# The first batch's softmax reciprocals turned from one repeated column instead of from a wide copy

## The chip, the cores and the metric

One core of one Trainium2 chip. The metric is device time in microseconds (us) of one execution. Lower is better. The engines are named as in the profile: PE is TensorE's products, PEld its weight loads, DVE is VectorE, ACT is ScalarE, POOL is GpSimd, SP is SyncE, which here only issues DMAs.

## The reference, cut to what matters

Three stages follow one another on 4 batches of 576 rows: attention with 8 heads of 64 columns, a gated feed-forward layer (the MoE names), and a spatial gating layer. The change lies in the attention alone:

```python
scores = scale * np.matmul(q_rot, k_rot.transpose(0, 1, 3, 2))
scores = scores - np.max(scores, axis=-1, keepdims=True)
attn = np.exp(scores)
attn = attn / (np.sum(attn, axis=-1, keepdims=True) + 1e-09)
return np.matmul(attn, v).astype(np.float32)
```

The division by the row's sum is what matters here. The kernel does not divide the exponentials. It multiplies the finished product with v by the reciprocals of the sums.

## The kernel before, in words

**Units.** The attention is cut into 72 units, 18 for each batch and 9 for each four heads. An ordinary unit m is 128 rows of the queries for two heads. Units 4, 13, 22 and so on (m % 9 == 4) are tails: the last 64 rows of four heads. So the first batch is units 0 to 17, of which 4 and 13 are tails and 16 are ordinary.

**One unit, step by step** (function `unit`, line 314). PE forms the scores into PSUM (`scores`, L347, or L339 and L336 from the second batch on). DVE takes the negated row maximum of each of two heads (`top`, L351). ACT takes the exponentials with the row's sum beside them (`expo`, L356, two of them). ACT adds 1e-9 (`total`, L360), and DVE takes the reciprocals (`norm`, L363), two numbers for each of 128 rows, in `sm[:, 3, :]`. ACT then copies each reciprocal 64 times side by side into a 128 x 128 tile `rb` (`spread`, L367). PE transposes the exponentials into PSUM in two halves of 8 (`turn`, L376). ACT copies these to SBUF (`take`, L404, two of them). `turn_rest` transposes the rest, into a PSUM tile `u`: the last 128 columns of exponentials (L389) and the wide tile of reciprocals (L390). In a tail it is 8 small products against the identity instead (L386), 4 of them on reciprocals. DVE copies the result to SBUF (`take_rest`, L411, L409 in a tail). When two ordinary units, or a tail, are complete, PE multiplies by v (`values`, L418), and DVE multiplies that by the turned reciprocals (`gather`, L430).

**Two kinds of ordinary units.** After units 1, 6, 8, 10, 15 and 17 the product with v follows directly; call these value units. After the ten others (0, 2, 3, 5, 7, 9, 11, 12, 14, 16) the next unit's transposes follow; call these plain units.

**What sets the order.** The order of all instructions on each engine is written by a list scheduler in the kernel (class `Plan`, line 52). Each step has an engine, a planned cost, the steps that it waits for, a delay after them (0.12 unless given) and a rank. A step on PE whose kind differs from the one before costs 0.10 more (`SWITCH`). The planned costs around the change: `scores` 1.07, `top` 0.75, `expo` 0.93, `total` 0.20, `norm` 0.17, `spread` 0.26, each half of `turn` 0.27, each `take` 0.59 with 0.05 between, `turn_rest` 0.22 (0.55 in a tail), `take_rest` 0.42, `values` 2.3 or 2.9. ACT also converts weights (L169, L180) between these, and DVE does weights (L165 to L174) and the rotation of q and k (L258, L266).

**Fillers.** Up to the planned time 125, the planner puts products of the identity with itself, whose results nobody reads, into gaps that it sees on PE (`filler`, L678):

```python
n = min(int((t - begin - FILL_MARGIN) / FILL_US), FILL_MOST)
```

with a margin of 0.30, 0.22 for one filler product and at most 20 of them. In the trace one filler product is two instructions. The number is fixed when the kernel is built: on the chip PE executes all of them, whether or not it would have waited.

**After the first batch** the feed-forward layer of the batch before (`feed`, L514, L553) shares PE with the attention of the next, and from about 500 us the later stages (L699, L763) follow.

Of the kernel before, what the change touches and what calls it, by code (L numbers as in the profile page):

```python
# [22 lines left out]
NFC = DF // 128  # L23
NU = B * 18
NFIRST = 2
EXACT = NP
WB, GB, WB2, GB2 = 3, 2, 3, 2
RAW, ROT, VB, PFB, PTB, XTS = 2, 4, 2, 3, 2, 6
# [5 lines left out]
HEAD = slice(0, 64), slice(64, 128)  # L34
# [17 lines left out]
class Plan:  # L52
# [5 lines left out]
    def add(self, eng, us, fn, deps=(), rank=0.0, after=0.12, take=None, give=None, port=False, kind=None):  # L58
        s = Step(eng, us, fn, deps, rank, after, take, give, port, kind)
        self.steps.append(s)  # L60
        return s
# [52 lines left out]
def body(ctx: ExitStack, tc, qp, kp, vp, cs, mu_k, mu_r, w_k, w_v, w_r, w_in, w_sp, b_sp, w_out, out):  # L114
    nc = tc.nc
# [21 lines left out]
    ident = const.tile([128, 128], F32, name="ident")  # L137
# [77 lines left out]
    add = plan.add  # L215
# [5 lines left out]
    ropes, vloads, exps, turned, valued, xdone, stored = {}, {}, {}, {}, {}, {}, {}  # L221
# [23 lines left out]
    def prep(i):  # L245
# [5 lines left out]
        for z, k in [(z, k) for z in sides for k in (1, 0)]:  # L251
# [8 lines left out]
            def rope(k=k, z=z):  # L260
                x = t["raw", k]
                if i >= EXACT:
                    t[k] = x[:, 0, :]
# [11 lines left out]
            def low(k=k):  # L275
                t["lo", k] = at.tile([128, S], F32R, tag="rl", bufs=ROT, name=f"rl{i}_{k}")
                nc.vector.tensor_tensor(t["lo", k], t[k], raw(t["hi", k]), op=ALU.subtract)
                if k == 0:
# [11 lines left out]
                    need - 2.5, port=True)  # L290
            if i < EXACT:
                ropes["n", n] = done[z.start, k] = add("DVE", 0.15 + 0.62 * part, rope, [a] + last, need - 2.5, port=True)
# [21 lines left out]
    def unit(m):  # L314
        w = which(m)
        tail = len(w) == 2
        st = units[m] = {}
        g, k = divmod(m, 9)
# [5 lines left out]
        def scores(halves=(0, 1)):  # L324
# [3 lines left out]
            ps = st["s"]  # L328
            if w[0][0] >= EXACT:
                for u, (i, c) in enumerate(w):  # L330
# [38 lines left out]
        def turn(n, slot=None):  # L369

            if n == 0:
                st["t"] = ps_t.tile([128, 2, 8, 64], F32, tag="t", name=f"t{m}")
            for c in range(4):
                for h, r in enumerate(HEAD):
                    k = 64 * (h if tail else n) + 128 * c
                    nc.tensor.transpose(st["t"][:, h, 4 * n + c, :], st["p"][r, n, k:k + 128], ident[r, r])  # L376

        def turn_rest(slot):

            pt, p = ps_m.tile([128, 4, 128], F32, tag=f"m{slot}", name=f"u{m}"), st["p"]  # L380
            st["u"] = pt
            if tail:
                for u in range(2):
                    for k in range(2):
                        for j, r in enumerate(HEAD):
                            nc.tensor.matmul(pt[r, u, HEAD[k]], st["r"][r, u, :] if k else p[r, u, 512 - 512 * j:576 - 512 * j],  # L386
                                             ident[r, r], start=True, stop=True)
            else:
                nc.tensor.transpose(pt[:, 0, :], p.rearrange("p a b -> p (a b)")[:, 512:640], ident)  # L389
                nc.tensor.transpose(pt[:, 1, :], st["r"].rearrange("p a b -> p (a b)"), ident)  # L390

        def turned_to(u):
            d = into[u if tail else 0]
# [4 lines left out]
        def take(k):  # L398
            o = turned_to(k)
            if tail:  # L400
                o = o[:, 0:8, 256:320].rearrange("p (h c) q -> p h c q", h=2)
            else:
                o = o[:, 4 * k:4 * k + 4, 128 * part:128 * part + 128].rearrange("p c (h q) -> p h c q", h=2)
            nc.scalar.copy(o, st["t"][:, :, 4 * k:4 * k + 4, :])  # L404
# [38 lines left out]
                             m - 0.5)  # L443
        t = add("ACT", 0.2, total, [exps[m, 1]], m - 0.3)
        nm = add("DVE", 0.17, norm, [t], m - 0.3)
        sp = add("ACT", 0.26, spread, [nm], m - 0.3)
        late = [y for d in into for y in freed.get(d["n"] - PTB, [])]
        t = add("PE", 0.27, lambda slot: turn(0), [exps[m, 0]], m + -0.02, take="t", kind="s")
        turned[m, 0] = x = add("PE", 0.27, lambda: turn(1), [exps[m, 1], t], m + 0.05, kind="s")
        x = add("ACT", 0.59, lambda: take(1), [x] + late, m - 0.2, 0.05)  # L450
        x = add("ACT", 0.59, lambda: take(0), [x] + late, m - 0.2, give=t)
        turned[m, 1] = t = add("PE", 0.55 if tail else 0.22, turn_rest, [sp], m + 0.2, take="m", kind="t")
        y = add("DVE", 0.55 if tail else 0.42, take_rest, [t] + late, m - 0.2, give=t)
        for d in into:
            d["ev"] += [x, y]
        if part and k != 3 or tail:
# [3 lines left out]
            x = add("DVE", 0.49 if duo["cols"] > 256 else 0.42, gather, [v] + mixed.get(i - XTS, []), m + 0.5, give=v)  # L460
# [130 lines left out]
    for c in (0, 2, 4, 6, 1, 3, 5, 7, *range(8, 16)):  # L591
        k = c < 8
# [6 lines left out]
    for m in range(NU):  # L599
        for i, _ in which(m):  # L600
            while i not in ropes:
                prep(len(vloads))
        unit(m)
        for n, args in enumerate(early):
            if m == EARLY + int(EVERY * n):
                weight_steps(weight_early(*args), m + 12, [scored[m]])
        for i in range(B * NP):
            if i not in ropes and i >= ROT // 2 and max(which_last(i - ROT // 2)) <= m:
                prep(i)
        if m % 18 == 17:  # L610
            if m == NU - 1:
                second["close"] = close = add("SP", 0.0, lambda: open_second(), [x for x in plan.steps if x not in fed], 74, 0.1)
            n = len(plan.steps)
            for h in range(2):
                feed(m // 18, h)
            fed.update(plan.steps[n:])
# [101 lines left out]
    def receptance_raw(b, e, r):  # L718
        ps = wide(f"r{b}_{e}")
        sl = slice(e * 128, (e + 1) * 128)  # L720
        product(ps, [(wr[w][:, c, sl], xr[a][:, c, :]) for c in range(NP) for a, w in PARTS])
        nc.scalar.activation(two_half(r), two_bank(ps), AF.Sigmoid)
        return r

    firsts = {(0, e): receptance_raw(0, e, stage[0].tile([128, S], F32, tag=f"rr{e}", name=f"rr0_{e}"))
              for e in range(NFIRST)}
    ph1.close()
# [192 lines left out]
```

## Time and profile before

| | us |
|---|---|
| median of 3 runs | 767.26 (766.88 to 768.66) |
| the profiled execution's own time | 766.66 |
| its span | 764.9 |
| PE busy | 748.1 (98%) |
| DVE busy | 474.8 (62%) |
| ACT busy | 457.0 (60%) |

The span is the time between the first and the last instruction in the profiled execution. A busy PE is not a PE that does useful work: fillers count as busy.

### The profile page before, as it was taken

Reading aid. Unit: us, or ns where it says so; the run is one execution under the profiler, and the core shown is the slowest. Engines: PE = TensorE matmul, PEld = TensorE weight load, DVE = VectorE, ACT = ScalarE, POOL = GpSimd, SP = SyncE. Lnnn points to the kernel's source line nnn. Section 1 sums busy time; section 2 is a strip of 40 time slices with the busy share of each in tenths; the row PEclk is TensorE's granted clock in tenths of the full one; section 3 lists DMA queues with packets and bytes.
Section 4 is the critical chain, followed back from the end, with each engine's and each line's share of the span. In section 5 each row is a group of like instructions: output and inputs, shape, how many; then the busy total and the mean of one; then the engine's idle time right before and its main releaser. Section 6 shows DMA issues by size and latency. Waiting matters only on the chain.

```text
span 764.9 us, 15911 instructions
## 1 busy us (share of the span) xinstructions
PE 748.1 (98%) x6530; PEld 668.0 (87%) x6530; DVE 474.8 (62%) x881; ACT 457.0 (60%) x1045; POOL 109.0 (14%) x132
## 2 busy tenths in 40 slices
PE   8999999999999999999999999999999999999998
PEld 8777778798788888888798799999989999998997
DVE  5878888988977986886866445256363342545111
ACT  4678788887887877878877555236334232523221
POOL 2242434102121121022031000002020000101000
PEclk9999999999999999999999999999999999999999
DMA  8444541442461552443351067182202112010101
GB/s 292 149 131 145 178 132 49 146 135 81 151 211 27 182 178 93 152 144 117 108 184 45 18 215 248 63 272 70 63 1 82 44 47 78 17 32 1 63 1 63
DMA packets 35275, 84.23 MB, mean 110 GB/s; under 512 B 4545, under 2 KB 10433, under 8 KB 35202
## 3 DMA queue, kind: packets, MB, share of 16 engines
q1 hardware_dynamic: 34658, 82.63, 32.9%
q8 instruction: 51, 0.84, 0.5%
q10 hardware_dynamic: 544, 0.59, 0.3%
q14 instruction: 22, 0.18, 0.1%
HBM read 60.65 MB, written 22.55 MB: 109 GB/s over the span
## 4 chain that ended last, share of the span: by engine, by line
PE 92%; DVE 3%; ACT 3%; DMA 1%; issue 0%; POOL 0%; ACTq 0%; POOLq 0%
PE mv L553 13%; PE mk L514 13%; PE v L418 11%; PE sp L699 8%; PE r L699 7%; PE u L699 7%; PE hv L763 7%; PE o L699 7%; PE t L376 6%; PE s L339 5%; PE s L347 2%; ACT pt L404 2%; PE u L389 1%; PE s L336 1%; DMA raw<-qp 1%; PE I-119_120 L678 1%
## 5 line engine op out<-in xcount | busy, mean ns | idle before, releaser
L351 DVE TENSOR_REDUCE sm<-s 128x1 f32<-128x576 f32 x144 | 106.1, 751 | 27.3 <-PE s L339 19.1
L356 ACT ACTIVATE pf<-s,sm 128x576 f32<-128x576 f32 x144 | 106.7, 750 | 11.5 <-DVE sm L351 11.3
L553 PE MATMUL mv<-kh,wv 128*128 128x288 f32 x512 | 108.9, 299 | 0.5 <-DVE pt L411 0.5
L514 PE MATMUL mk<-x,wk 128*128 128x288 f32 x768 | 109.1, 298 | 0.0
L514 PEld LDWEIGHTS mk<-x,wk 128*128 128x128 f32 x768 | 102.7, 188 | 1.2 <-DVE xt L430 0.5
L404 ACT COPY pt<-t 128x512 f32<-128x512 f32 x144 | 77.9, 589 | 37.3 <-PE t L376 36.6
L418 PE MATMUL v<-pt,vt 128*64 128x256 f32 (+1 forms) x640 | 84.7, 411 | 6.2 <-ACT pt L404 5.0
L553 PEld LDWEIGHTS mv<-kh,wv 128*128 128x128 f32 x512 | 83.8, 188 | 2.1 <-issue 1.2
L418 PEld LDWEIGHTS v<-pt,vt 128*64 128x64 f32 x640 | 44.4, 136 | 36.0 <-ACT pt L404 7.8
L553 PE MATMUL mv<-kl,wv 128*128 128x288 f32 x256 | 75.6, 295 | 0.0
L376 PEld LDWEIGHTS t<-ident,pf 64*128 64x128 f32 x1152 | 52.0, 138 | 24.3 <-issue 8.3
L376 PE MATMUL t<-ident,pf 64*128 64x64 f32 x1152 | 63.7, 229 | 0.9 <-ACT pf L356 0.9
L699 PE MATMUL sp<-ws,vn 128*128 128x288 f32 x384 | 53.9, 295 | 0.0
L699 PE MATMUL r<-xr,wr 128*128 128x288 f32 x384 | 52.5, 296 | 1.2 <-ACT vs L559 1.2
L699 PE MATMUL o<-g,wo 128*128 128x288 f32 x384 | 52.9, 296 | 0.5 <-ACT os L822 0.5
L699 PEld LDWEIGHTS r<-xr,wr 128*128 128x128 f32 x384 | 51.7, 188 | 1.8 <-ACT vs L559 1.5
L699 PEld LDWEIGHTS sp<-ws,vn 128*128 128x128 f32 x384 | 52.4, 188 | 0.7
L699 PEld LDWEIGHTS o<-g,wo 128*128 128x128 f32 x384 | 51.7, 188 | 1.4 <-ACT os L822 1.2
L699 PE MATMUL u<-x,wi 128*128 128x288 f32 x384 | 52.0, 296 | 0.0
L699 PEld LDWEIGHTS u<-x,wi 128*128 128x128 f32 x384 | 51.6, 188 | 0.3
L553 PEld LDWEIGHTS mv<-kl,wv 128*128 128x128 f32 x256 | 48.2, 188 | 0.0
L258 DVE TENSOR_TENSOR raw<-raw,cst 128x1152 f32<-128x1152 f32 (+1 forms) x34 | 43.3, 1280 | 7.0 <-DMA raw<-kp 5.4
(414 smaller groups left out, 1256.4 us busy)
## 6 DMA issues: line engine op xcount, KB each, us to landing
raw<-kp SPq DMA_DIRECT2D x15, 576.0 KB, 3.8
raw<-qp SPq DMA_DIRECT2D x15, 576.0 KB, 4.7
vt<-vp SPq DMA_DIRECT2D x16, 320.0 KB, 3.6
xd<-xt SPq DMA_DIRECT2D x16, 288.5 KB, 3.6
vd<-vs SPq DMA_DIRECT2D x32, 144.0 KB, 2.0
v<-vd SPq DMA_DIRECT2D x16, 288.0 KB, 2.8
out<-os SPq DMA_DIRECT2D x15, 288.0 KB, 2.1
wi<-wd SPq DMA_DIRECT2D x8, 512.0 KB, 4.8
```

The lines of the kernel that those rows point to most:

```text
L258: nc.vector.tensor_tensor(t["raw", k][:, :, z], t["raw", k][:, :, z], cst[:, :, z], op=ALU.mult)
L339: nc.tensor.matmul(ps[j][:, h, :HALF], t[a, 0][r, 128 * c:128 * c + 128], t[b, 1][r, x], **f)
L347: nc.tensor.matmul(o, q[r, 128 * c:min(128 * c + 128, S)], k[r, h * HALF:(h + 1) * HALF], start=True, stop=True)
L351: nc.vector.tensor_reduce(st["sm"][:, 0, j:j + 1], st["s"][j][:, :, :HALF], axis=AX.XY, op=ALU.max, negate=True)
L356: nc.scalar.activation(st["p"][:, j, :].rearrange("p (a b) -> p a b", a=2), st["s"][j][:, :, :HALF], AF.Exp, bias=st["sm"][:, 0, j:j + 1], ...
L376: nc.tensor.transpose(st["t"][:, h, 4 * n + c, :], st["p"][r, n, k:k + 128], ident[r, r])
L404: nc.scalar.copy(o, st["t"][:, :, 4 * k:4 * k + 4, :])
L418: nc.tensor.matmul(pv[HEAD[j], z], v[:, 4 * j + c if c < 4 else 8 + j, :], pt[:, 4 * j + c if c < 4 else 8, z], start=c == 0, stop=c == 4)
L514: nc.tensor.matmul(ps[:, :HALF], wk[w][:, c, fc * 128:(fc + 1) * 128], a[:, c, :], start=k == 0, stop=k == 11)
L553: nc.tensor.matmul(xs["v", dc][:, :HALF], wv[w][:, fc, dc * 128:(dc + 1) * 128], a, start=k == 0, stop=k == 23)
L699: nc.tensor.matmul(ps[:, h, :HALF], w, a[:, h * HALF:(h + 1) * HALF], start=m == 0, stop=m == n - 1)
L763: nc.tensor.matmul(ps[:, :FS], x[a][:, d, c:c + 128], wi[w][:, d, FS:], start=k == 0, stop=k == 11)
```

## The change

For units 0 to 17 the wide copy on ACT is not made. `turn_rest` waits for the reciprocals themselves. In an ordinary unit the one transpose of the 128 x 128 tile is replaced by two products, one for each head. The stationary operand of each is the single column of reciprocals, read 64 times with a step of zero (128 rows, 64 columns), and the moving operand is the 128 x 128 identity. Each writes 64 of the 128 partitions. In a tail the 4 small products on reciprocals stay as they are, but for the operand, which is the repeated column. The planned cost of `turn_rest` in these ordinary units goes from 0.22 to 0.33. Units 18 to 71 keep the copy and the transpose.

```diff
+NARROW = 18
...
                     for k in range(2):
                         for j, r in enumerate(HEAD):
-                            nc.tensor.matmul(pt[r, u, HEAD[k]], st["r"][r, u, :] if k else p[r, u, 512 - 512 * j:576 - 512 * j],
+                            x = st["sm"][r, 3, u:u + 1].to_broadcast([64, 64]) if "r" not in st else st["r"][r, u, :]
+                            nc.tensor.matmul(pt[r, u, HEAD[k]], x if k else p[r, u, 512 - 512 * j:576 - 512 * j],
                                              ident[r, r], start=True, stop=True)
             else:
                 nc.tensor.transpose(pt[:, 0, :], p.rearrange("p a b -> p (a b)")[:, 512:640], ident)
-                nc.tensor.transpose(pt[:, 1, :], st["r"].rearrange("p a b -> p (a b)"), ident)
+                if "r" in st:
+                    nc.tensor.transpose(pt[:, 1, :], st["r"].rearrange("p a b -> p (a b)"), ident)
+                else:
+                    for j, r in enumerate(HEAD):
+                        nc.tensor.matmul(pt[r, 1, :], st["sm"][:, 3, j:j + 1].to_broadcast([128, 64]), ident, start=True, stop=True)
...
-        sp = add("ACT", 0.26, spread, [nm], m - 0.3)
+        sp = nm if m < NARROW else add("ACT", 0.26, spread, [nm], m - 0.3)
...
-        turned[m, 1] = t = add("PE", 0.55 if tail else 0.22, turn_rest, [sp], m + 0.2, take="m", kind="t")
+        turned[m, 1] = t = add("PE", 0.55 if tail else 0.33 if m < NARROW else 0.22, turn_rest, [sp], m + 0.2, take="m", kind="t")
```

## Rows read from the trace of the kernel before

**Rows 1.** The page: busy time of the engines, and granted clock in 40 slices
```profile
PE 748.1 (98%) x6530; PEld 668.0 (87%) x6530; DVE 474.8 (62%) x881; ACT 457.0 (60%) x1045; POOL 109.0 (14%) x132
...
PEclk9999999999999999999999999999999999999999
```
**Rows 2.** Windows: length, then busy time of PE, PEld, DVE, ACT, POOL
```profile
10.00:110.00 100.00, 97.10 (x977) 75.09 (x976) 84.49 (x157) 77.08 (x190) 32.78 (x27) 1.00 0.48 158
110.00:440.00 330.00, 323.61 (x3283) 276.92 (x3282) 254.70 (x483) 259.47 (x649) 56.95 (x53) 1.00 0.37 121
```
**Rows 3.** Windows, the fillers of L678 alone: length, PE, PEld
```profile
10.00:110.00 100.00, 36.02 (x265) 32.03 (x266) 1.00 0.48 158
```
**Rows 4.** Chain of waits, 66 to 84 us: start, us on the chain, what
```profile
68.18 0.26 PE t L376 x8
...
68.46 1.08 ACT pt L404 x2
...
69.59 2.38 PE v L418 x20
...
73.63 0.26 PE u L389
73.89 0.11 PE u L390
74.00 1.79 PE I-996_997 L678 x16
...
83.46 0.64 PE u L386 x16
```
**Rows 5.** Timeline of the plain unit 11 (start, us, engine, line), idle before in brackets
```profile
73.67 1.07 ACT L404 COPY pt<-t 128x512 f32<-128x512 f32 x2 [1.60 <-PE t L376]
...
74.63 0.76 ACT L356 ACTIVATE pf<-s,sm 128x576 f32<-128x576 f32 x1
...
75.71 0.46 PE L376 MATMUL t<-ident,pf 64*128 64x64 f32 x8
```
**Rows 6.** The tile rb: instructions, ns min/median/max, first and last start
```profile
L367 ACT COPY rb<-sm x72: 274/297/302, 14.4 to 429.7; 128x128 f32<-128x128 f32 x72
...
L386 PE MATMUL u<-ident,rb x64: 218/218/218, 36.8 to 409.7; 64*64 64x64 f32 x64
```
**Rows 7.** Waits from 8 to 122 us: total us, times, longest
```profile
ACT rb L367 <- DVE sm L363: 4.9, 7, 1.6
...
PE t L376 <- ACT pf L356: 0.9, 2, 0.7
PE u L390 <- ACT rb L367: 0.4, 1, 0.4
```
**Rows 8.** Timeline around the value unit 1
```profile
21.33 0.30 ACT L367 COPY rb<-sm 128x128 f32<-128x128 f32 x1 [1.57 <-DVE sm L363]
...
22.05 0.42 DVE L411 COPY pt<-u 128x256 f32<-128x256 f32 x1
...
22.78 0.44 PE L418 MATMUL v<-pt,vt 128*64 128x256 f32 x2
```
**Rows 9.** Fillers of L678: one group a line, instructions in it, ns, first and last start
```profile
L678 PE MATMUL I-249_250<-ident x24: 275/275/275, 16.0 to 18.6; 128*128 128x128 f32 x24
...
L678 PE MATMUL I-872_873<-ident x18: 275/275/275, 64.0 to 65.9; 128*128 128x128 f32 x18
...
L678 PE MATMUL I-388_389<-ident x16: 275/275/275, 27.0 to 28.7; 128*128 128x128 f32 x16
```
**Rows 10.** Chain of waits in the plain unit 16
```profile
100.87 1.56 PE I-1358_1359 L678 x14
```
**Rows 11.** The page: weight loads of L418, busy us, mean ns, idle before
```profile
L418 PEld LDWEIGHTS v<-pt,vt 128*64 128x64 f32 x640 | 44.4, 136 | 36.0 <-ACT pt L404 7.8
```
**Rows 12.** Timeline: one cast of a weight on ACT
```profile
98.47 0.60 ACT L180 CAST wv<-I-1244_1245 128x512 fp32r<-128x512 f32 x1
```

## The prediction

> **What bounds the kernel now.** I read the page first, then windows, then the chain of waits inside the first batch, and last the timeline beside that chain. On the page PE is busy 98% of the span and its granted clock is full in all 40 slices [rows 1], so PE looks like the bound everywhere. The windows split this. From 110 to 440 us PE is busy 323.61 of 330 us with real work [rows 2]; what an earlier stretch gains is carried through there. From 10 to 110 us, which holds the first batch, PE is busy 97.10 of 100 us, but 265 of its instructions are fillers [rows 2, 3]. One filler instruction takes 1.79 / 16 = 0.112 us on the chain [rows 4], so fillers are 265 x 0.112 = about 30 us of this stretch. PE is full there because the planner has filled it.
>
> The chain shows two patterns. In a value unit it goes from the transposes to ACT's two takes (1.08 us) and on to the product with v [rows 4]: `turn_rest` and its fillers lie beside the takes. In a plain unit it stays on PE: 0.26 for L389, 0.11 for L390, then 16 filler instructions [rows 4]. There ACT is a little ahead: the takes start at 73.67, the first exponential ends at 74.63 + 0.76 = 75.39, and PE starts the transposes that need it only at 75.71, after the fillers [rows 5]. So in a plain unit PE, fillers included, has about 0.3 us less room than ACT. Only twice does PE wait for an exponential there, 0.9 us in all [rows 7].
>
> **The copy that goes.** 18 copies of 0.297 us [rows 6] are 5.3 us of ACT. Nearly all of it is hidden. ACT itself idles 4.9 us ahead of these copies, waiting for the reciprocals [rows 7]. In a value unit such as unit 10 the takes follow the transposes at once [rows 4], so the copy before them costs nothing. The exception is unit 1, where the reciprocals come late: the copy starts at 21.33, PE waits 0.4 us for it (the only such wait), and v starts at 22.78 [rows 7, 8]. Without the copy the takes start earlier, and the next thing late is DVE's copy of `u`, which runs from 22.05 to 22.47 behind a maximum and need not move [rows 8]. So v could start near 22.48: **-0.3 us**. If the cover in the other units were gone, each copy would be worth its 0.3 us; that is the second case below.
>
> **The products that come.** One transpose of 0.11 us [rows 4] becomes two products. A product here is two instructions, as a filler product is, so four instructions with 64 stationary and 128 moving columns. No row has this form. From below: the small products of a tail take 0.64 / 16 = 0.04 us each with 64 stationary and 64 moving columns [rows 4]. From above: a filler instruction with 128 and 128 columns takes 0.112 us. The nearest row is the product with v, which has the same 64-column load: 2.38 / 20 = 0.119 us for 256 moving columns [rows 4]. At the full clock of 2.4 GHz 256 columns are 0.107 us, so there is 0.012 over; 128 columns then give 0.053 + 0.012 = 0.066 us. Four are 0.26 us, so **+0.15 us** for each of 16 ordinary units (ends: 0.16 - 0.11 = +0.05, and 0.45 - 0.11 = +0.34). The tails keep their forms [rows 6] and cost nothing more.
>
> The Trainium skill (TensorE: Matmul & The Clock Gate, Back-to-back issue gap) puts a step at columns / 2.4 + 2.5 ns, which for 256 columns is 109 ns against the row's 119, so the measured step is longer. By the page four steps would be 0.22 us and the sum below lower by 8 x 0.04 = 0.3 us.
>
> In the six value units the +0.15 lies beside the takes: in unit 10 PE spends 0.26 + 0.11 and some fillers of 0.112 while ACT needs 1.08 [rows 4]; I count nothing. DVE's copy of `u` becomes ready 0.15 later, but it is planned behind a maximum of the next unit, which ends at about that time; nothing there either. The reciprocals are now read by PE out of `sm`, which has four buffers; the next writer is four units later and does not wait. No DMA, no POOL step and no SP step is added or removed.
>
> **The fillers that go.** The planned cost of `turn_rest` rises by 0.11, and the gap behind it shrinks. In a plain unit, from the end T of the second half of `turn`, the planner has the takes from T + 0.12 to T + 1.35, the exponential until T + 2.28, the next transposes at T + 2.40, and `turn_rest` until T + 0.22 + 0.10. The gap is 2.08, and (2.08 - 0.30) / 0.22 = 8.09 gives 8 fillers, the x16 of the trace [rows 4, 9]. With 0.33 the gap is 1.97, and 7.59 gives 7. One filler fewer is 2 x 0.112 = 0.224 us on PE, more than the 0.15 that came.
> - Units 2, 3, 5, 11 and 12 have x16, one shape of gap. Unit 9 has x18 [rows 9], from a longer gap; half of the possible lengths lose one filler, and I take it as lost. Six units: 6 x (0.152 - 0.224) = **-0.43**.
> - Unit 0 has x24 [rows 9]; the copy and a cast stand ahead of its takes in the plan, so its gap shrinks by 0.26 + 0.11 = 0.37, near two fillers: 0.152 - 0.448 = **-0.3**.
> - Unit 16 has x14 [rows 10], already the 7 fillers: its `turn_rest` was held up by the copy in the plan, and no more than the standard gap 1.97 comes back. None goes: **+0.15**.
> - Units 7 and 14 are where PE waits for an exponential (0.9 us, [rows 7]): what PE gains or loses goes into that wait, 0.
>
> **The sum**: -0.3 - 0.43 - 0.3 + 0.15 = **-0.9 us** in the first batch, carried through by the full PE behind it [rows 2]. Against the profiled execution's own 766.66 that is 765.8; that execution is 0.6 below the median 767.26, so I forecast **766.4**. With the ends of the product's price, over eight units on PE's path: 8 x (0.05 - 0.15) gives 765.6, 8 x (0.34 - 0.15) gives 767.9. And the list scheduler may swap steps anywhere once times shift; PE is idle 6.4 us from 110 to 440 us [rows 2], of which I let 1 us come or go.
>
> **The rivals.**
> 1. *The freed ACT time shortens the plan itself.* The takes come earlier in the plan wherever the copy stood ahead of them, the gaps shrink again, and each of the eight plain units on PE's path loses a second filler: another 8 x 0.224 = 1.8, so 764.6. It needs ACT to keep up, which has about 0.3 us of room a unit [rows 5], so it can go once and not further. For it: ACT is busy 77% of this stretch [rows 2]. Against it: 4.9 us of idle ahead of the copies. If the copy cost its full time everywhere, 18 x 0.297 would give 762.
> 2. *A cast slips ahead of the takes* (slower). ACT's free time is offered to whichever step is ready, and weight casts of 0.60 us [rows 12] are always about. One that lands between the transposes and the takes of a value unit delays v by its whole length, since that path is the chain [rows 4]. Each costs 0.6; from five such places on (-0.9 + 3.0 = +2.1) the kernel is slower by more than 0.2%: 769.4. Fewer places, with the narrow products at 0.112 us, end alike.
> 3. *The narrow loads are not hidden.* Each of four loads would then add its 0.136 us [rows 11] to a step: 4 x 0.136 = +0.54 for an ordinary unit. On the eight units of PE's path that is 4.4, and in the six value units, with room for perhaps 0.3, 1.5 more: 771.4. Against it: 20 loads of 0.136 are 2.7 us, and the whole group took 2.38 [rows 4, 11], so they ran beside the products. The Trainium skill (TensorE: Matmul & The Clock Gate, Part 3, What overlaps and what doesn't) has loads overlap products in flight only where the row groups differ, and here all rows are used; by that rule this rival would hold. The trace disagrees: the group with v, 0.119 us a step, uses all rows too.
> 4. *Nothing moves*: products and fillers cancel, and the gain of unit 1 is lost in DVE's queue: 767.3.
>
> **How the numbers follow.** A measurement of this kernel tells a change from none at about 0.2%, or 1.5 us: below 765.7 is faster, above 768.8 slower. My forecast 766.4 has 0.40, and with its bounds it reaches a little past 765.7, 0.06 of it. Rival 1 has 0.30, rival 2 0.13, rival 3 0.03, rival 4 0.14. Faster: 0.30 + 0.06 = 0.36. Slower: 0.13 + 0.03 = 0.16. Same: the rest, 0.48. The range runs from rival 1 with 1 us of swapped steps below it, 763.4, to just under rival 2, 769.0; the full price of the copy, rival 3 and the worst of rival 2 are left out.
>
> **What would show each step.** The four new instructions should start about 0.066 us apart: 0.04 or 0.112 would be the ends, 0.2 rival 3. The x16 groups of fillers should read x14 (rival 1: x12), x24 should read x20. PE's busy time from 10 to 110 us should stay near 97 us. The start of v in unit 1 should come 0.3 us earlier. ACT's takes should still follow the transposes at once in value units; a cast between them is rival 2. What would make the whole prediction wrong is an order of the first batch so different that these groups cannot be matched, or a gain after 110 us, where the change touches nothing.

## The result and the profile after

The changed kernel takes 774.82 us against 767.07 for the kernel before in the same session: ratio 1.0102, interval 1.0084 to 1.0119. It is 7.75 us **slower**, where I had forecast 0.9 us faster, and it lies outside the range.

The page and the windows of the changed kernel, in the form of [rows 1, 2]:

```profile
PE 753.9 (98%) x6572; PEld 669.7 (87%) x6572; DVE 479.3 (62%) x881; ACT 454.2 (59%) x1027; POOL 110.1 (14%) x132
...
PEclk9999999999999999999999999999999999999999
...
10.00:110.00 100.00, 97.72 (x957) 73.45 (x957) 82.70 (x150) 71.58 (x165) 31.92 (x26) 1.00 0.47 153
110.00:440.00 330.00, 322.43 (x3287) 275.73 (x3286) 260.67 (x488) 260.31 (x652) 58.41 (x54) 1.00 0.37 122
```

The clock is full as before. PE is as busy as before in both stretches, so busy time does not show the loss: the same stretch simply holds less work. The chain does. Here is a plain unit of the changed kernel, unit 11 (start, us on the chain, what), beside the same one before [rows 4]:

```profile
76.46 0.24 PE t L377 x8
76.70 0.26 PE u L391
76.96 0.37 PE u L396 x4
77.33 1.76 PE I-982_983 L684 x14
79.09 0.39 PE t L377 x8
```

L391 is the unchanged transpose. The narrow products, L396, take 0.37 us where the one transpose took 0.11. By the shape of a product I mean the rows and columns of the array that it uses, which the profile writes as 128*64 for a narrow product and 128*128 for a filler or a transpose in `u`. The fillers did go from 16 instructions to 14, as worked out, but these 14 take 1.76 us, hardly less than the 1.79 of the 16 before. At 0.112 each they should take 1.57, so **0.19 us** is lost as the fillers begin. The narrow form thus costs 0.26 + 0.19 = 0.45 us, and the filler that went gives back 0.22.

A value unit, unit 8, in the changed kernel and then in the kernel before:

```profile
60.31 0.24 PE t L377 x8
60.55 0.26 PE u L391
60.81 0.37 PE u L396 x4
61.18 0.88 PE I-788_789 L684 x6
62.06 0.14 issue
62.19 0.40 PE v L424
```

```profile
58.35 0.26 PE t L376 x8
58.61 0.02 issue
58.63 1.08 ACT pt L404 x2
59.71 0.07 issue
59.78 0.41 PE v L418
```

Before, the chain ran through ACT's takes. After, the narrow products and the fillers behind them outlast the takes, the product with v waits for PE's own queue, and there is no cover. From the end of the scores to the start of v it was 59.78 - 58.35 = 1.43 us and is 62.19 - 60.31 = 1.88 us.

Where the loss stands along the execution is seen in the starts of `turn_rest`, from the first unit behind the first batch (unit 18) to the last unit of all (unit 71). These rows are, in this order, from the kernel before and the changed one (count, ns, first and last start in us):

```profile
L389 PE MATMUL u<-ident,pf x48: 270/328/330, 109.5 to 434.2; 128*128 128x128 f32 x48
```

```profile
L391 PE MATMUL u<-ident,pf x48: 272/328/331, 114.7 to 441.5; 128*128 128x128 f32 x48
```

At unit 18 the changed kernel is 114.7 - 109.5 = 5.2 us behind, at unit 71 it is 441.5 - 434.2 = 7.3. So 2.1 us came after the first batch, in units that the change leaves as they were. Two things had to be told apart: the price of the products (theory P), and the price of another order, which the list scheduler writes once a step is gone from its list (theory O).

### The profile page after: what moved, and what is told of

It reads as the page before. It is cut to its first block, busy times and chain, and to the rows that moved or that the text cites. A ratio compares the mean times of both kernels' runs of the same rounds, so it can differ in the third digit from the quotient of the medians.

```text
span 772.5 us, 15967 instructions
## 1 busy us (share of the span) xinstructions
PE 753.9 (98%) x6572; PEld 669.7 (87%) x6572; DVE 479.3 (62%) x881; ACT 454.2 (59%) x1027; POOL 110.1 (14%) x132
## 4 chain that ended last, share of the span: by engine, by line
PE 91%; DVE 4%; DMA 2%; ACT 1%; issue 1%; SPq 0%; ACTq 0%; DVEq 0%
PE mv L559 13%; PE mk L520 13%; PE v L424 10%; PE sp L705 8%; PE r L705 7%; PE u L705 7%; PE hv L769 7%; PE o L705 7%; PE t L377 6%; PE s L340 5%; PE s L348 2%; DMA raw<-qp 2%; PE u L391 2%; PE s L337 1%; DVE raw L259 1%; DVE sm L352 1%
## 5 line engine op out<-in xcount | busy, mean ns | idle before, releaser
L259 DVE TENSOR_TENSOR raw<-raw,cst 128x1152 f32<-128x1152 f32 (+1 forms) x34 | 45.4, 1338 | 7.1 <-DMA raw<-kp 5.4
```

What stands on the lines that cost most here:

```text
L259: nc.vector.tensor_tensor(t["raw", k][:, :, z], t["raw", k][:, :, z], cst[:, :, z], op=ALU.mult)
```

## The experiments

The diffs are against the changed kernel, except where a run says otherwise.

### Products alone: the order of before, with the narrow products

The step of the copy keeps its place and its planned cost but does nothing, so every engine has the order, and PE the fillers, of the kernel before.

```diff
-        sp = nm if m < NARROW else add("ACT", 0.26, spread, [nm], m - 0.3)
+        sp = add("ACT", 0.26, spread if m >= NARROW else lambda: None, [nm], m - 0.3)
-        ... add("PE", 0.55 if tail else 0.33 if m < NARROW else 0.22, turn_rest, [sp], m + 0.2, take="m", kind="t")
+        ... add("PE", 0.55 if tail else 0.22, turn_rest, [sp], m + 0.2, take="m", kind="t")
```

> The order and the fillers of the kernel before on every engine; the wide copy is left out in units 0 to 17 (its place in the plan is kept) and the narrow products are executed. Theory P (the narrow products cost what the trace after shows: from the first of the two transposes in u to the second filler 0.95 us against 0.50, because the array changes between 128 and 64 columns): 16 x 0.45 = 7.2 slower than before, less what hides in the value units and unit 1, so 771.5 to 774.5. Theory O (the products cost the 0.15 each that I had forecast, and the new order made by the planner costs the rest): about 767 to 769.

Measured: 771.34 against 766.69, ratio 1.0058 (1.0043 to 1.0073), just under the span of theory P and far over theory O's. Its `turn_rest` starts, and its unit 11:

```profile
L391 PE MATMUL u<-ident,pf x48: 270/328/330, 114.3 to 439.0; 128*128 128x128 f32 x48
...
76.26 0.26 PE u L391
76.52 0.37 PE u L396 x4
76.89 1.98 PE I-983_984 L684 x16
```

Unit 18 starts 4.8 us later than before and unit 71 4.8 us: with the old order the whole loss is in the first batch and nothing is added behind it. The 16 fillers take 1.98, the 1.79 of before and the same 0.19.

The records also show why it is 4.8 us and not 16 x 0.45 = 7.2. From one start of `turn_rest` to the next, nine units are 0.43 to 0.45 us longer than before: the plain units 2, 3, 5, 9, 11, 12 and 16, and the value units 8 and 15, which have six filler instructions. The value units 6, 10 and 17, which have four, are 0.21 to 0.22 longer and unit 14 is 0.18. Unit 7, and units 0 and 1 taken together, lose nothing.

### The new order alone: the order of the changed kernel, with one transpose

```diff
-                    for j, r in enumerate(HEAD):
-                        nc.tensor.matmul(pt[r, 1, :], st["sm"][:, 3, j:j + 1].to_broadcast([128, 64]), ident, start=True, stop=True)
+                    nc.tensor.transpose(pt[:, 1, :], ident, ident)
```

> The order and the fillers of the changed kernel; in place of the narrow products one 128 x 128 transpose, of the identity instead of the reciprocals, so what is written there is not used rightly: the turning of the reciprocals is left out in the ordinary units 0 to 17. Theory P: 16 x 0.45 comes back from 774.8, so 767 to 769. Theory O: the order keeps its price, 772 or more.

Measured: 769.08 against 766.69, ratio 1.0028 (1.0019 to 1.0038). The products are most of the loss, but 2.4 us stay that are not theirs: theory O holds a part. The starts of `turn_rest`:

```profile
L391 PE MATMUL u<-ident,pf x48: 270/329/330, 109.4 to 436.3; 128*128 128x128 f32 x48
```

At unit 18 this order is 0.1 us ahead of the kernel before (109.4 against 109.5), and by unit 71 it is 2.1 us behind (436.3 against 434.2).

### The copies alone

The edits of the last two runs together (shown in part): the planned steps and costs of before, no copy, and one transpose.

```diff
+        sp = add("ACT", 0.26, spread if m >= NARROW else lambda: None, [nm], m - 0.3)
...
+                    nc.tensor.transpose(pt[:, 1, :], ident, ident)
```

> The order and the fillers of the kernel before, the wide copy left out in units 0 to 17, and one 128 x 128 transpose of the identity where the wide copy was transposed: the turning of the reciprocals is left out in the ordinary units. What the 18 copies alone are worth. The prediction's step (nearly all hidden): -0.3, so 766.3 to 767.2. If ACT set the pace in the first batch: up to -5, so 762.

Measured: 765.9 against 766.69, ratio 0.9991 (0.9982 to 1.0001): 0.8 us at the median, and the interval touches no change. Nothing like 5. The copies were hidden, as the prediction said. Against this run, the one with the new order and the same products is 769.08 - 765.9 = 3.2 us slower, which is the order by itself, its fillers included. In both runs the transpose of the identity waits for no reciprocals. That lets unit 1 of the one with the new order start its `turn_rest` at 19.7 us against 21.6 in this one, but by unit 6 both are at 47.5, so nothing of it is left. With every wait in place the order costs nearly the same: the changed kernel is 7.75 us slower than before and the old order with the narrow products 4.65, which leaves 3.1.

From unit 18 to unit 71 the new order took 436.3 - 109.4 = 326.9 us, and this run 434.4 - 109.6 = 324.8:

```profile
L391 PE MATMUL u<-ident,pf x48: 270/328/330, 109.6 to 434.4; 128*128 128x128 f32 x48
```

So 2.1 us of the order's price lie there. PE's waits from 110 to 445 us, of the run with the new order and then of this one (total us, times, longest):

```profile
PE v L423 <- ACT pt L409: 5.0, 6, 1.2
PE mk L519 <- DVE pt L414: 1.4, 2, 0.7
...
PE mk L519 <- DVE xt L435: 0.3, 1, 0.3
PE u L393 <- ACT rb L368: 0.2, 1, 0.2
```

```profile
PE v L423 <- ACT pt L409: 4.1, 6, 0.8
PE u L393 <- ACT rb L368: 1.2, 2, 0.6
```

The rows left out are alike in both but for 0.2 us. PE waits 0.9 us more for takes, and 1.7 us in new places (products of the feed-forward layer that stand behind a wait for DVE), and 1.0 less for copies; with those 0.2 that is 1.4 of the 2.1 us. The rest is not shown by a wait. Part may be changes of shape on PE: counted in the records from 110 to 445 us there are 169 with the new order and 162 with the old. At the 0.15 us by which L391's 0.26, behind transposes of 64 rows, is over the 0.11 of the transpose that follows it, seven more would be about 1 us, an estimate that no run tests.

### A change of shape fewer: the narrow products first

As the first experiment, but the two narrow products stand ahead of the transpose of the exponentials, so that what follows them up to the fillers is of one shape.

```diff
-                    nc.tensor.transpose(pt[:, 0, :], p..., ident)
                     for j, r in enumerate(HEAD):
                         nc.tensor.matmul(pt[r, 1, :], st["sm"][:, 3, j:j + 1].to_broadcast([128, 64]), ident, start=True, stop=True)
+                    nc.tensor.transpose(pt[:, 0, :], p..., ident)
```

> As the run with the order of before and the narrow products, but the narrow products stand ahead of the transpose of the exponentials in u, so that the array goes from the transposes with 64 rows to 64 columns and then stays at 128 x 128 into the fillers: one change of shape fewer. If the price is in the changes of shape: 0.15 to 0.25 less for each of 16 units, 2.5 to 4 us faster than that run. If it is in the number of instructions: the same as that run.

Measured: 769.1, ratio 1.0028 (1.0017 to 1.0039), 2.2 us faster than with the products behind. Its unit 11:

```profile
74.65 0.24 PE t L377 x8
74.89 0.37 PE u L396 x4
75.26 0.26 PE u L397
75.52 1.79 PE I-983_984 L685 x16
```

The same instructions, and the 16 fillers are back at 1.79: the 0.19 us belonged to the change from 64 to 128 columns ahead of them. The change back to 128 columns now falls on L397, which takes 0.26 as it did behind the transposes of 64 rows, so one change of shape is saved and not both. 2.2 / 16 = 0.14 us a unit is a little under what I expected. The value unit 8 saves all 0.19 (1.69 us from the end of the scores to v, against 1.88 with the products behind), but unit 7, where PE waits for an exponential, saves nothing.

### Fewer fillers

Three kernels with one edit, two filler products fewer in each gap and the single ones gone, the order of the rest unchanged: the kernel before, the one with the narrow products first, and the changed one.

```diff
-FILL, FILL_US, FILL_MARGIN, FILL_MOST = 125.0, 0.22, 0.3, 20
+FILL, FILL_US, FILL_MARGIN, FILL_MOST = 125.0, 0.22, 0.75, 20
```

> The kernel before with FILL_MARGIN 0.75 in place of 0.30: two filler products fewer in each gap, the single ones gone; the order of all other instructions is the same. If the fillers of the first batch are what PE executes too much of (about 0.3 us a plain unit ahead of ACT), 1.5 to 2.5 us faster than before: 764 to 765.3. If they hide behind ACT and DVE: the same as before. If the clock falls with fewer of them: slower, with a granted clock under 1.0.

> The run with the narrow products ahead of the transpose and the order of before, with FILL_MARGIN 0.75. If the price of the products (2.3 us over before in that run) is paid only because PE still executes as many fillers behind them: the fewer fillers take it back, 765 to 766.5. If it is paid on the way of the data itself: about 769 less what the kernel before gains from the same margin.

> The changed kernel with FILL_MARGIN 0.75. If what the products cost is PE time in front of fillers that did not shrink with it: 16 units lose up to 0.45 us each and most of 5 us comes back, 770 or less; what remains over before is the order (2 to 3 us). If the products sit on the way of the data: 773 or more.

Measured, against 766.78: the kernel before 765.01 (0.9976, 0.9966 to 0.9986), as expected; the narrow products first **763.7** (0.9960, 0.9945 to 0.9976), better than expected; the changed kernel 769.09 (1.0026, 1.0011 to 1.0040), as expected. Against the kernel before of its own session, the run with the narrow products first goes from 2.4 us slower to 3.1 faster, so 5.5 come off; the changed kernel goes from 7.75 slower to 2.3, so 5.4 come off; and only 1.8 come off the kernel before. The products' price was PE time queued in front of fillers, not time on the way of the data. What remains of the changed kernel over the best is 769.09 - 763.7 = 5.4 us. That is as much as the order (3.2) and the change of shape (2.2) had cost above, but it is no check of them: the mean clock of the changed kernel was 0.995 to 0.999 in these runs against 0.997 to 1.000, and in its two runs at 0.999 it took 766.24 and 767.30.

The kernel that leaves out the copies, puts the narrow products first, keeps the old order and has fewer fillers beats both kernels. That its lead over the kernel before with the same margin (1.3 us) is the copies' own is not shown: with that margin the clock of the latter fell in its first batch. The windows, first of the kernel before with margin 0.75, then of the best (the figure behind POOL's is the granted clock):

```profile
20.00:30.00 10.00, 7.99 (x61) 5.44 (x61) 7.83 (x18) 5.75 (x15) 1.28 (x1) 0.83 0.49 170
```

```profile
20.00:40.00 20.00, 18.32 (x189) 13.17 (x191) 18.53 (x37) 12.72 (x30) 6.09 (x4) 1.00 0.48 170
```

### Fewer still

FILL_MARGIN 1.2 with the narrow products first, and then fillers only up to the planned time 20 (FILL = 20.0), with the narrow products first and in the kernel before.

> The run with the narrow products first, the order of before and FILL_MARGIN, now 1.2: some two filler products fewer in each gap again. If PE still stands ahead of ACT by its fillers: up to 1 us faster than with 0.75 (763.7). If ACT and DVE now set the pace, the same; if the clock falls in more stretches, slower.

> The narrow products first, the order of before, and fillers only up to the planned time 20. It bounds what the fillers after that are worth: without a fall of the clock 762 to 763; with the clock at 1.2 GHz in part of the first batch it is slower than 764, and the granted clock from 20 to 110 us shows where.

> The kernel before with fillers only up to the planned time 20, beside the run with narrow products and the same. The copies and the products against each other without fillers between: if the narrow form is worth more than the copies' 0.8 us where nothing is queued behind it, this one is 1 us or more slower than that run; if the products' time shows, it is faster.

Measured, against 766.68: margin 1.2 gives 763.97 (0.9978, 0.9951 to 1.0004), from 762.24 to 770.36 in its runs and no better than 0.75. Its runs part by the clock: the four with a mean clock of 0.999 took 762.24 to 763.24, the two with 0.989 took 770.0 and 770.36. Few fillers give 771.88 (1.0058, 1.0038 to 1.0079) with the narrow products and 772.06 (1.0073, 1.0045 to 1.0101) in the kernel before. The windows of the narrow one with few fillers, and then three of the kernel before with few fillers:

```profile
20.00:40.00 20.00, 15.67 (x166) 9.77 (x163) 19.04 (x36) 13.89 (x32) 4.01 (x4) 1.00 0.45 152
40.00:60.00 20.00, 15.13 (x140) 9.52 (x136) 15.51 (x25) 12.87 (x29) 8.83 (x8) 0.91 0.49 165
60.00:80.00 20.00, 16.85 (x162) 10.45 (x161) 16.69 (x31) 14.69 (x35) 4.09 (x4) 0.91 0.24 84
80.00:110.00 30.00, 23.88 (x213) 14.64 (x213) 24.07 (x47) 22.48 (x54) 9.83 (x8) 0.85 0.40 131
```

```profile
40.00:60.00 20.00, 14.13 (x124) 9.07 (x122) 16.05 (x28) 14.43 (x35) 7.82 (x8) 0.89 0.46 160
60.00:80.00 20.00, 15.75 (x150) 9.82 (x146) 15.99 (x30) 14.94 (x38) 4.75 (x5) 0.94 0.23 73
80.00:110.00 30.00, 23.59 (x222) 15.15 (x224) 26.31 (x51) 24.86 (x62) 9.95 (x9) 0.89 0.41 138
```

In the narrow one the clock is still full from 20 to 40 us and falls to 0.85 to 0.91 in the three windows after it: PE spends part of them at the lower of its two levels, 1.2 and 2.4 GHz. So some of the fillers pay for themselves, but not all: with two products fewer in each gap the kernel before and the one with the narrow products first were faster. The last comparison, copies against products without fillers between, stays open: 0.2 us apart, with both intervals wider than that and the clock different in each.

## Why the prediction was wrong

- **The sum that was measured.** Each run is taken against the kernel before of its own session: the changed kernel +7.75 us, the narrow products in the old order 771.34 - 766.69 = +4.65, the new order without them 769.08 - 766.69 = +2.39, the old order with neither them nor the copies 765.9 - 766.69 = -0.79. So the products cost 7.75 - 2.39 = 5.4 in the new order and 4.65 + 0.79 = 5.4 in the old, the new order costs 3.1 to 3.2, and the copies give 0.8. That the products' price is the same in both orders is the check; the sum 5.4 + 3.2 - 0.8 = 7.8 is made of the same four numbers. The prediction had -0.9 for all of it.
- **"Four are 0.26 us, so +0.15 us for each of 16 ordinary units"**: this step failed, by its size and by its upper end. The four take 0.37, so +0.26, and the fillers after them start 0.19 late: 0.45 against an upper end of 0.34. The 0.45 stands in nine of the 16 units, plain and value, with the old order. Two errors made it. I took the products with v, 2.38 / 20 = 0.119 us, as steps one after another. In the changed kernel's records the four narrow instructions start in two pairs: by 0.11 us after the first one two have started, and by 0.17 all four. The two of a pair use different halves of the columns and run side by side, and v's 0.119 is half of a pair's time, 2.38 / 10 = 0.238. The filler's 0.112 us for 128 columns, one at a time, was the nearer row, and I had it as the far end. And I priced the instructions without the change of shape on either side of them.

```profile
76.89 0.33 PE L396 MATMUL u<-ident,sm 128*64 128x128 f32 x2
```

This is the timeline of the changed kernel up to 77.0 us. The count in the same view up to 77.5 us is x4.

- The Trainium skill's step of columns / 2.4 + 2.5 ns (TensorE: Matmul & The Clock Gate, Back-to-back issue gap), weighed there, would be 0.056 us for 128 columns, an estimate; the page gives it for a product alone and says that it counts too little when the columns are few. One filler instruction takes 0.112 at the full clock, twice that, so the rule is further off than my step was.
- **"In the six value units ... I count nothing"** failed with it: in unit 8 the fillers end after the takes, and all 0.45 us shows; with the old order units 8 and 15 show all of it, and 6, 10 and 17 about half.
- **"The fillers that go"** held in most units: 14 where there were 16 in units 2, 3, 11 and 12, and in the changed kernel unit 0 has x20, unit 9 x16, unit 16 its x14, as worked out. It failed in unit 5, which was to go from 16 to 14 and went to 20; the chain runs over DVE there, so those are not seen to cost. Unit 17 was not foreseen either: 12 fillers where there were 4, on the chain. The rows of unit 5, before and after, and of unit 17 after:

```profile
L678 PE MATMUL I-603_604<-ident x16: 275/275/275, 43.1 to 44.7; 128*128 128x128 f32 x16
```

```profile
L684 PE MATMUL I-587_588<-ident x20: 275/275/377, 43.9 to 46.1; 128*128 128x128 f32 x20
```

```profile
109.27 1.55 PE I-1399_1400 L684 x12
110.82 0.14 issue
110.95 2.38 PE v L424 x20
```

- **"The copy that goes"** held in that nearly all of it was hidden: -0.3 forecast, -0.8 with an interval that touches none. The place that I gave for the -0.3 did not hold. In unit 1 of the changed kernel v starts at 23.06, 1.63 us after the reciprocals begin (21.43), and before it was 1.64 (22.78 and 21.14): what the copy gave the longer products took, and PE waits 0.9 us for the reciprocals themselves. Even without the products (the run of the copies alone) v starts there at 22.84, no earlier than before.
- **"The list scheduler may swap steps anywhere ... I let 1 us come or go"** was too little: the order cost 3.1 to 3.2 us, 2.1 of it between units 18 and 71. This was the second step that failed. The sign could not be read from the profile before, and neither could the size: PE's idle 6.4 us there bounds what a swap can gain, not what it can lose.
- **The rivals.** Rival 1 (a second filler goes) did not happen in the plain units with x14. Rival 2 (a cast ahead of the takes) is not what made it slower: the chain of the value unit has PE in that place. Rival 3 does not add up: 4.4 + 1.5 over the forecast 766.4 is 772.3, not 771.4. It said the loads of the narrow products would not be hidden, by the Trainium skill's rule on row groups (TensorE: Matmul & The Clock Gate, What overlaps and what doesn't). Adding loads up does not settle that, neither here (four of 0.134 us against a group of 0.37) nor for v in the prediction, since the loads lie beside one another: all four take 0.20 us. The starts say more. The first two loads begin with their products, at 76.89. The other two begin by 76.96 in the records, while those products are still in flight, and all use the 128 rows, so for them the trace disagrees with that rule. What is not hidden is a load of the next shape: the first filler's begins at 77.26 together with its product, where before it began 0.10 us ahead (73.73 and 73.83). So part of what I call the change of shape is rival 3 one step later, at the filler's load, and no run parts the two. The loads of all units and of unit 11, its first fillers, and the same two rows of the kernel before:

```profile
L396 PEld LDWEIGHTS u<-ident,sm x64: 132/134/135, 15.4 to 108.9; 128*64 128x64 f32 x64
...
76.89 0.20 PEld L396 LDWEIGHTS u<-ident,sm 128*64 128x64 f32 x4
77.26 0.52 PEld L684 LDWEIGHTS I-982_983<-ident 128*128 128x128 f32 x4 [0.17 <-issue]
...
77.26 0.49 PE L684 MATMUL I-982_983<-ident 128*128 128x128 f32 x2
```

```profile
73.73 0.30 PEld L678 LDWEIGHTS I-996_997<-ident 128*128 128x128 f32 x2
73.83 0.28 PE L678 MATMUL I-996_997<-ident 128*128 128x128 f32 x1
```

## What to carry to other kernels

In this kernel a small product on a busy PE cost its own steps plus the changes of shape on either side, so price one from a row of the same width that runs one at a time, and put it next to work of its own shape. Fillers, or any queue fixed when the kernel is built, turn an underpriced step into time: where the planned cost rises by 0.11 and the real one by 0.45, the wait that would have absorbed it has been filled. And where a scheduler writes the order, dropping a step is two changes; keep the step's place with nothing in it to measure the one, and the new order with the old work to measure the other.

## What the runs showed of the hardware that was not expected

- A change from products with 64 columns to 128 cost about 0.19 us at the start of the next group: 14 fillers in 1.76 us and 16 in 1.98, against 16 in 1.79 where no change stands ahead. The load of the first filler is then not fetched ahead of it (both at 77.26, against 73.73 and 73.83).
- Two products on different column halves start together (two of the four narrow ones by 0.11 us, all four by 0.17), so a row's mean per instruction can be half of what one costs alone.
- Without the fillers behind the planned time 20 the granted clock of the kernel before was 0.89 to 0.94 in the three windows from 40 to 110 us, and that cost more than leaving the fillers out gives: it went from 766.68 to 772.06.
